# A two-layer decode kernel: output weights of layer 0's last pairs loaded behind the values, the output product one pair behind, the MLP loads recut, no tile context

## The chip, the cores and the metric

The kernel runs on one core of one Trainium2 chip. The metric is the device time of one execution in microseconds (us). Comparisons are between medians of several runs of each kernel; the profile is one execution, recorded by the hardware profiler.

## The reference

Two layers with the same weights, each attention and then an MLP, for one token:

```python
x = A_x                                     # 1 x 1 x 640, bf16
for layer in range(2):
    # attention: 32 heads of 192; of 32768 cached keys the last W = 4096 count
    h = layernorm(x)
    q = (h @ wq) per head                   # wq: 640 x 6144
    p = softmax(q @ k[:, -W:].T * 192**-0.5)
    x = x + concat(p @ v[:, -W:]) @ wo      # wo: 6144 x 640
    # MLP: 1536 wide
    h = layernorm(x)
    x = x + (sigmoid(h @ w_gate) * (h @ w_up)) @ w_down
```

## The kernel before

Work goes by pairs of heads, 16 pairs in each layer. On the host the tensors are laid out so that a pair needs two loads of the same size, 128 rows of 28416 bytes (3552 KB): `a` (from `ua`) holds the pair's query weights and keys, `b` (from `ub`) its values (the first `VE` columns, 3072 KB) and its output weights (the last `WOE` columns, 480 KB). SBUF has seven slots of that size and one region of 3072 KB (`mreg`), which holds MLP weights in the first MLP and the last, and the values of pair 1 in between.

One pair in `step(p, prev)`: `Q` (query projection, L351), `QK` (scores, L366), the softmax (`soft`, `expo`), then for the pair before `PVmm` (values, L420), and `PVout`: a turn of the result (L435), its scaling on DVE (L438, to `oTb`) and the product with the output weights (L445), which adds to `yT`. `ET` (L396 to L405) turns the exponentials of the new pair. In layer 0 the middle of this is a loop of seven turns with two pairs each; in layer 1 the first pairs have an order written out by hand.

Not everything is loaded twice. In layer 0 the loads of pairs 0, 14 and 15 and the keys of pair 1 go to slots that are kept (`KEPT`), and layer 1 begins with these pairs (14, 15, 0, 1), so that its first work needs few new bytes.

All big loads go out on SP's queue, in one fixed order, `seq`. For a layer it is a0, a1, b0, a2, b1, a3, b2 and so on; the last pair's values come in three parts (`b1`, then `b0` twice). Behind layer 0 come the MLP's weights (gate in two parts `wg`, up in two parts `u1`, `u2`, down in two `d1`, `d2`), the values of pair 1 for layer 1 in three parts (`va`, `vb`, `vc`), the keys of layer 1's pair 2 in two parts (`a0`), pair 1's output weights (`wom`) and then layer 1's pairs. While the program is written, `prefetch` puts loads on SP as far as it can: it stops at the first entry of `seq` whose slot is still busy or whose event has not been written yet. Each load waits on SP for the last readers of what it overwrites, and everything behind it on SP waits too.

In layer 0 the keys of pair p go to slot p % 2 and the values to slot 2 + p % 2, apart from the kept pairs 0 and 1 (keys to 4 and 6, values of 0 to slot 5). A key slot comes free at the end of `QK`, a value slot at the end of `PVout`:

```python
            elif not (l == 0 and ("b", p) in KEPT):
                release(sv)
```

`emit` and `emit_pe` write each engine's instructions with their semaphore waits. After the block of all engines come a clearing of semaphores, a barrier and `finish`, which makes the last product as its weights land, writes the output and clears six semaphores on SP. All of it is inside a tile context and a critical section of it.

Of the kernel before, what the change touches and what calls it, by code (L numbers as in the profile page):

```python
# [9 lines left out]
ALU = mybir.AluOpType  # L10
# [34 lines left out]
class _Prog:  # L45

    def __init__(self):
        self.ops = {e: [] for e in ("pe", "dve", "act", "dma", "adma")}
        self.cnt = {e: 0 for e in ("pe", "dve", "act")}
        self.dcnt = {}  # L50
        self.seg = None
# [55 lines left out]
def decode_kernel(ctx: ExitStack, tc: tile.TileContext, cx: bass.AP, ua: bass.AP, ub: bass.AP,  # L107
                  wg_d: bass.AP, wu_d: bass.AP, wd_d: bass.AP, out: bass.AP):
    nc = tc.nc
# [3 lines left out]
    ctx.enter_context(tc.tile_critical(name="decode", no_gpsimd_drain=True))  # L113
# [24 lines left out]
    sh = sb("sh", [P, 6 * DC + 4 + FC], BF16)  # L138
# [3 lines left out]
    oTb = sh[:, 6 * DC:6 * DC + 3]  # L142
    hT = sh[:, 6 * DC + 4:6 * DC + 4 + FC]
# [26 lines left out]
    rm = {n: res("m_" + n) for n in "abc"}  # L170
    MOFF = {"a": (0, 5 * FW), "b": (5 * FW, 12 * FW), "c": (12 * FW, ME)}
# [32 lines left out]
    seq += [("wg", 0), ("wg", 1), ("u1",), ("u2",), ("d1",), ("d2",), ("va",), ("vb",), ("vc",)]  # L204
    tail = stream(1, range(2, 14))
    assert tail[0] == ("a", 1, 2)
    seq += [("a0", 0), ("a0", 1), ("wom",)] + tail[1:]
    seq += [("fg",), ("fu",), ("fd", 0), ("fd", 1), ("fd", 2)]
    seq_pos = [0]
    busy = set()  # L210
# [3 lines left out]
    GH = 5  # L214
# [10 lines left out]
    def try_load(it):  # L225
        k = it[0]
        if k in ("a", "b"):
            s = (A_SLOT if k == "a" else B_SLOT)[it[1]][it[2]]
            if not take(s):
                return False  # L230
            pg.dma(q_dma(slot(s, 0, UNIT), (ua if k == "a" else ub)[it[2]]), f"s{s}", wr=[rslot[s]])
        elif k == "b1":
            s = B_SLOT[it[1]][it[2]]
            if not take(s):
                return False
            n = len(pg.ops["dma"])
            pg.dma(q_dma(slot(s, NB * DH, UNIT - NB * DH), ub[it[2]][:, NB * DH:]), f"s{s}", wr=[rslot[s]])
            ev_done["b1"] = list(pg.ops["dma"][n]["deps"].items())
        elif k == "b0":
            s = B_SLOT[it[1]][it[2]]  # L240
            o = it[3] * NHALF
            pg.dma(q_dma(slot(s, o, NHALF), ub[it[2]][:, o:o + NHALF]), f"bh{it[3]}", wr=[res(f"bh{it[3]}")], extra=ev_done["b1"])
        elif k == "a0":
            if f"a14_{it[1]}" not in ev_done:
                return False
            s = A_SLOT[1][2]
            o0, o1 = ((0, A0CUT), (A0CUT, UNIT))[it[1]]
            pg.dma(q_dma(slot(s, o0, o1 - o0), ua[2][:, o0:o1]), f"a0{it[1]}", wr=[res(f"a0{it[1]}")] + ([rslot[s]] if it[1] else []),
                   extra=[ev_done[f"a14_{it[1]}"]])
        elif k == "wg":  # L250
            f0, f1 = ((0, GH), (GH, FC))[it[1]]
            pg.dma(q_dma(mreg(f0 * FW, (f1 - f0) * FW), wg_d[:, f0 * FW:f1 * FW]), f"wg{it[1]}", wr=[[rm["a"]], [rm["b"]]][it[1]])
        elif k == "u1":
            pg.dma(q_dma(mreg(12 * FW, 7 * FW), wu_d[:, 0:7 * FW]), "u1", wr=[rm["c"]])
        elif k == "u2":
            if "gate0" not in ev_done:
                return False
            pg.dma(q_dma(mreg(0, 5 * FW), wu_d[:, 7 * FW:]), "u2", wr=[rm["a"]])
        elif k == "d1":
            if "gate1" not in ev_done:  # L260
                return False
            pg.dma(q_dma(mreg(5 * FW, 7 * FW), wdp(0, 7)), "d1", wr=[rm["b"]], extra=[ev_done["gate0"]])
        elif k == "d2":
            if "up0" not in ev_done:
                return False
            pg.dma(q_dma(mreg(12 * FW, 5 * FW), wdp(7, 12)), "d2", wr=[rm["c"]])
        elif k in ("va", "vb", "vc"):
            if "down0" not in ev_done:
                return False
            o0, o1 = MOFF[k[1]]  # L270
            pg.dma(q_dma(mreg(o0, o1 - o0), ub[PM][:, o0:o1]), k, wr=[rm[k[1]]])
        elif k == "wom":
            if "QM" not in ev_done:
                return False
            pg.dma(q_dma(slot(A_SLOT[1][PM], 0, WOE), ub[PM][:, VE:UNIT]), "wom", wr=[res("wom")], extra=[ev_done["QM"]])
        elif k == "fg":
            pg.dma(q_dma(mreg(0, 12 * FW), wg_d), "fg", wr=[rm["a"], rm["b"], rm["c"]])
        elif k == "fu":
            if not take(U_SLOT):
                return False  # L280
            pg.dma(q_dma(slot(U_SLOT, 0, 12 * FW), wu_d), f"s{U_SLOT}", wr=[rslot[U_SLOT]])
        else:
            if it[1] == 0 and not take(D_SLOT):
                return False
            c0, c1 = WFIN[it[1]]
            pg.dma(q_dma(slot(D_SLOT, c0 * D, (c1 - c0) * D), wdp(c0, c1)), f"wf{it[1]}", wr=[rslot[D_SLOT]] if it[1] == 0 else [])
        return True
# [50 lines left out]
    def attention(l, xi):  # L338
# [6 lines left out]
        def Q(p, y):  # L345
            sa = A_SLOT[l][p]

            def f(t):
                for i, c0 in enumerate((0, P, 2 * P)):
                    for c in range(DC):  # L350
                        ins = t.matmul(qe[:, i:i + 1], lhsT=slot(sa, c * 2 * DH + c0, P), rhs=xq[:, c:c + 1], start=(c == 0), stop=(c == DC - 1))  # L351
                return ins
            ev = pg.op("pe", f, rd=[res("xq"), rslot[sa]] + ([res("a00")] if l == 1 and p == 2 else []), ex=[rb[3]])
            pg.op("dve", lambda v: v.tensor_tensor(out=qs[:, y], in0=qe[:, 0:3].unsqueeze(2).to_broadcast([P, 3, 32]), in1=mask3, op=ALU.mult),  # L354
                  rd=[res("cst")], wr=[res(f"qs{y}")], ex=[rb[3]])
            return ev
# [51 lines left out]
        def PVmm(p, z):  # L408
# [3 lines left out]
            for h in (1, 0) if half else (0, 1):  # L412
                vt = (mreg(h * NB * DH, NB * DH) if inm else slot(sv, h * NB * DH, NB * DH)).rearrange("p (t d) -> p t d", t=NB)
                for part in (0, 1) if half and h == 0 else (None,):
# [8 lines left out]
                    rV = list(rm.values()) if inm else [rslot[sv]] + ([] if part is None else [res(f"bh{part}")])  # L423
# [4 lines left out]
        def PVout(p, z):  # L428
            inm = l == 1 and p == PM
            sv = None if inm else B_SLOT[l][p]  # L430

            def tm(t):
                for c in range(3):
                    for sg in range(2):
                        ins = t.matmul(oT3[:, c:c + 1], lhsT=o8_sb[:, sg, c:2 * DH:3], rhs=mask2[:, sg:sg + 1], start=(sg == 0), stop=(sg == 1))  # L435
                return ins
            pg.op("pe", tm, rd=[res("o8sb0"), res("o8sb1"), res("cst")], ex=[rb[6]])
            pg.op("dve", lambda v: v.tensor_scalar(out=oTb, in0=oT3[:, 0:3], scalar1=Rn[z], scalar2=None, op0=ALU.mult),  # L438
                  rd=[res(f"Rn{z}0"), res(f"Rn{z}1")], wr=[res("oTb")], ex=[rb[6]])
            wo = slot(A_SLOT[1][PM], 0, WOE) if inm else slot(sv, VE, WOE)  # L440

            def im(t):
                for j in range(DC):
                    for c in range(3):
                        ins = t.matmul(yT[:, j:j + 1], lhsT=wo[:, c * D + j * P:c * D + (j + 1) * P], rhs=oTb[:, c:c + 1],  # L445
# [3 lines left out]
            pg.op("pe", im, rd=[res("oTb")] + ([res("wom"), rslot[sa]] if inm else [rslot[sv]]), ex=[rb[7]])  # L449
            if inm:  # L450
                release(sa)
            elif not (l == 0 and ("b", p) in KEPT):
                release(sv)

# [4 lines left out]
        def step(p, prev):  # L459
# [6 lines left out]
            PVout(prev, prev % 2)  # L466
# [14 lines left out]
        if l == 0:  # L481
# [9 lines left out]
            p = NPAIR - 1  # L491
        else:
            Q(14, 0)
            ln_sq(xi)
            mark("a14_0", QK(14, 0, ks=(0,)))
            mark("a14_1", QK(14, 0, ks=(1, 2)))
            Q(15, 1)
            ln_rstd(K2_ATT, eps_a, srs_c, res("srs"))
            mark("QM", Q(PM, 0))
            QK(15, 1, 1)  # L500
# [3 lines left out]
            Q(0, 1)  # L504
            soft(1)
            expo(1)
            QK(0, 1)
# [6 lines left out]
            QK(PM, 0)  # L514
# [10 lines left out]
            p = 13  # L525
        PVmm(p, p % 2)
        PVout(p, p % 2)
# [10 lines left out]
    def mlp(l, xi):  # L538
# [23 lines left out]
        if last:  # L562
            proj(0, range(FC), g_of, 0, [rm["a"], rm["b"], rm["c"]])
        else:
            mark("gate0", proj(0, range(GH), g_of, 0, [rm["a"]]))
            mark("gate1", proj(0, range(GH, FC), g_of, 0, [rm["b"]]))
# [9 lines left out]
        HS = (0, 7, FC)  # L576
        if last:
            u_of = lambda fb: slot(U_SLOT, fb * FW, FW)
            ru = [[rslot[U_SLOT]]] * 2
        else:  # L580
            u_of = lambda fb: mreg(12 * FW + fb * FW, FW) if fb < 7 else mreg((fb - 7) * FW, FW)
            ru = [[rm["c"]], [rm["a"]]]
        ubank = (1, 6)
        proj(ubank[0], range(0, 7), u_of, 1, ru[0])
        if not last:
            mark("up0")
        proj(ubank[1], range(7, FC), u_of, 1, ru[1], 7)
# [10 lines left out]
        for i in range(2):  # L598
            c0, c1 = HS[i], HS[i + 1]
            wd = mreg((5 if i == 0 else 12) * FW, (c1 - c0) * D)  # L600
# [7 lines left out]
            pg.op("pe", f, rd=[res(f"hT{i}"), rm["b"] if i == 0 else rm["c"]], ex=[rb[7]])  # L608
        mark("down0")
        return residual(xi)  # L610

    def finish():
# [10 lines left out]
        nc.sync.dma_start(out.rearrange("b s (g n) -> (b s g) n", g=NRG), o_row[0:32 * NRG:32]).then_inc(tail_sem["out"], 16)  # L623
        nc.sync.wait_ge(tail_sem["out"], 16)
        for t_ in tail_sem.values():
            nc.sync.sem_clear(t_)
# [90 lines left out]
    with nc.Block() as block:  # L717
# [3 lines left out]

        @block.vector
# [76 lines left out]
```

## Time and profile before

| | before |
|---|---|
| median of 3 runs | 524.4 us (523.97 to 524.91) |
| the profiled execution | 524.21 us |
| its span, first to last instruction | 522.4 us |
| PE matmul busy | 276.6 us (53%) |
| DVE, ACT busy | 97.9 us, 87.9 us |
| SP's load queue | 219.13 MB, 98.5% of 16 engines' time |
| granted TensorE clock, mean | 0.597 |

The span is cut into 40 slices of 13 us for the rows of busy tenths and GB/s. The profile's chain of work that ended last follows each step back to what released it; a DMA stands in it from its issue to its landing, with its time in other loads' wake. The landing of a load is told by 16 marks in the trace, one for each DMA engine; a wait for the load ends with the last of them. L numbers are lines of the kernel of each run.

### The profile page before, as it was taken

The page shows a single profiled execution, that of the slowest core. Times are in us where ns is not written, and L with a number is a line of the kernel's source. Part 1 is how long each engine was busy: PE and PEld are TensorE (multiplying, and loading weights), DVE is VectorE, ACT ScalarE, POOL GpSimd, SP SyncE. Part 2 cuts the span into 40 slices and gives each one's busy share as a digit, 9 for nine tenths or more (in the row PEclk, how much of TensorE's full clock was granted, in tenths as well). Part 3 has the DMA queues.
Part 4 walks back from the last instruction along what each step waited for, and adds up shares of the span by engine and source line. Part 5 has one row for each costly group of instructions (what it writes and reads, how often), then busy time and mean ns, then how long its engine had stood idle before and what let it go on. Part 6 is the DMA issues. An engine that isn't in the chain of part 4 may idle for free.

```text
span 522.4 us, 8445 instructions
## 1 busy us (share of the span) xinstructions
PE 276.6 (53%) x3716; PEld 139.8 (27%) x3716; DVE 97.9 (19%) x372; ACT 87.9 (17%) x171; POOL 0.2 (0%) x4
## 2 busy tenths in 40 slices
PE   0635354544545354545565768677554544545365
PEld 0222122222222122212224434333222222222134
DVE  1212111112011111111111232332211112011111
ACT  0122111210122102210120032222211210122110
POOL 0000000000000000000000000000000000000000
PEclk9967665756665655555555556866666656555555
DMA  8999999999999999999999999999999999999995
GB/s 351 429 434 430 434 428 429 433 429 439 429 425 435 429 435 429 431 435 429 429 415 371 366 440 430 434 423 434 430 429 429 431 433 435 429 429 431 424 426 225
DMA packets 11115, 219.45 MB, mean 420 GB/s; under 512 B 1368, under 2 KB 1368, under 8 KB 2904
## 3 DMA queue, kind: packets, MB, share of 16 engines
q1 hardware_dynamic: 10952, 219.13, 98.5%
q8 instruction: 13, 0.21, 0.2%
q10 hardware_dynamic: 144, 0.06, 0.1%
q14 instruction: 6, 0.05, 0.0%
HBM read 219.18 MB, written 0.00 MB: 420 GB/s over the span
## 4 chain that ended last, share of the span: by engine, by line
DMA 73%; PE 18%; DVE 4%; SPq 1%; issue 1%; ACT 1%; ACTq 0%; DVEq 0%
DMA big<-in_ub_dram 61%; PE o L420 8%; DMA big<-in_wd_dram 7%; DMA big<-in_wu_dram 5%; PE scores L366 3%; PE bank L403 2%; PE bank L445 1%; SPq L182 1%; PE bank L396 1%; ACT e_sb L390 1%; DVE sc L405 1%; PE bank L382 1%; DVE et_sb L400 1%; DVE sc L376 1%; DVE sh L438 1%
## 5 line engine op out<-in xcount | busy, mean ns | idle before, releaser
L420 PE MATMUL o<-big,et_sb 128*2 128x384 bf16 x1024 | 86.3, 511 | 54.8 <-DMA big<-in_ub_dram 54.7
L366 PE MATMUL scores<-big,qs 128*32 128x512 bf16 x744 | 83.8, 620 | 10.3 <-DVE qs L354 9.8
L379 ACT ACTIVATE diag<-cst,sc 128x128 f32<-128x128 bf16 x32 | 12.8, 401 | 263.0 <-DVE sc L376 255.4
L351 PE MATMUL bank<-sh,big 128*128 128x1 bf16 x480 | 17.7, 166 | 71.6 <-DMA big<-in_ua_dram 71.3
L420 PEld LDWEIGHTS o<-big,et_sb 128*2 128x2 bf16 x1024 | 29.2, 113 | 98.6 <-DMA big<-in_ub_dram 63.9
L376 DVE TENSOR_REDUCE sc<-scores 128x1 f32<-128x1024 f32 x31 | 38.0, 1224 | 80.4 <-PE scores L366 80.4
L382 PE MATMUL bank<-diag,sc 128*128 128x128 f32 x64 | 23.3, 462 | 47.9 <-ACT diag L379 47.9
L390 ACT ACTIVATE e_sb<-scores,sc 128x1024 bf16<-128x1024 f32 x31 | 37.3, 1204 | 41.3 <-DVE sc L385 39.4
L425 ACT CAST o_sb<-o 128x384 bf16<-128x384 f32 x64 | 30.4, 477 | 78.0 <-PE o L420 77.9
L366 PEld LDWEIGHTS scores<-big,qs 128*32 128x32 bf16 x744 | 24.2, 134 | 44.4 <-issue 31.4
L351 PEld LDWEIGHTS bank<-sh,big 128*128 128x128 bf16 x480 | 15.7, 105 | 74.6 <-DMA big<-in_ua_dram 73.2
L382 PEld LDWEIGHTS bank<-diag,sc 128*128 128x128 f32 x64 | 14.6, 285 | 73.6 <-ACT diag L379 71.9
L400 DVE CAST et_sb<-bank 128x64 bf16<-128x64 f32 x32 | 7.2, 225 | 127.4 <-PE bank L396 127.4
L354 DVE TENSOR_TENSOR qs<-bank,cst 128x96 bf16<-128x96 f32 x32 | 8.2, 258 | 103.7 <-PE bank L351 103.6
L445 PE MATMUL bank<-sh,big 128*128 128x1 bf16 x480 | 17.4, 165 | 16.4 <-DVE sh L438 16.4
L403 PE MATMUL bank<-sc 128*128 128x2 f32 x64 | 15.5, 312 | 14.5 <-DVE sc L401 14.5
L445 PEld LDWEIGHTS bank<-sh,big 128*128 128x128 bf16 x480 | 14.7, 100 | 19.0 <-DVE sh L438 18.6
L383 DVE TENSOR_REDUCE sc<-bank 128x2 f32<-128x128 f32 x32 | 9.3, 292 | 43.5 <-PE bank L382 43.5
L403 PEld LDWEIGHTS bank<-sc 128*128 128x128 f32 x64 | 12.8, 249 | 17.3 <-DVE sc L401 17.3
L396 PEld LDWEIGHTS bank<-cst,e_sb 128*128 128x128 bf16 x256 | 9.1, 103 | 23.2 <-ACT o_sb L425 16.8
L396 PE MATMUL bank<-cst,e_sb 128*128 128x8 bf16 x256 | 11.9, 170 | 5.6 <-ACT e_sb L390 5.6
L405 DVE RECIPROCAL sc<-bank 64x1 f32<-64x1 f32 x64 | 10.6, 165 | 19.5 <-PE bank L403 18.5
(60 smaller groups left out, 98.5 us busy)
## 6 DMA issues: line engine op xcount, KB each, us to landing
big<-in_ua_dram SPq DMA_DIRECT2D x27, 3552.0 KB, 30.0
big<-in_ub_dram SPq DMA_DIRECT2D x26, 3552.0 KB, 28.5
big<-in_ub_dram SPq DMA_DIRECT2D x2, 2016.0 KB, 16.3
big<-in_ub_dram SPq DMA_DIRECT2D x4, 768.0 KB, 18.5
big<-in_ua_dram SPq DMA_DIRECT2D x1, 2048.0 KB, 12.7
big<-in_wg_dram SPq DMA_DIRECT2D x1, 1920.0 KB, 23.3
big<-in_wu_dram SPq DMA_DIRECT2D x1, 1920.0 KB, 27.4
big<-in_ua_dram SPq DMA_DIRECT2D x1, 1504.0 KB, 8.4
```

Source lines behind the costliest of these rows:

```text
L351: ins = t.matmul(qe[:, i:i + 1], lhsT=slot(sa, c * 2 * DH + c0, P), rhs=xq[:, c:c + 1], start=(c == 0), stop=(c == DC - 1))
L366: ins = t.matmul(sc_x[1 + b][32 * j:32 * j + 32, :], lhsT=qs[:, y, k, :], rhs=slot(sa, WQE + k * W + (4 * b + j) * 512, 512), start=(k == ...
L376: pg.op("dve", lambda v: v.reduce_max(out=mx, in_=sc_x[0][:], axis=AX.X), wr=[res("mx")], ex=sc_x[3:5])
L379: pg.op("act", lambda a: a.mul(out=diag[:], in_=ident, mul=mx), rd=[res("cst"), res("mx")], wr=[res("diag")])
L382: pg.op("pe", lambda t: t.matmul(dmx[:, 0:P], lhsT=ones_f, rhs=diag[:], start=True, stop=True), rd=[res("diag"), res("ones")], ex=[rb[2]])
L390: pg.op("act", lambda a: a.activation(out=e_sb[:], in_=sc_x[0][:], func=ACT.Exp, bias=nbias, scale=srs_c, accum_out=rowsum), rd=[res("nbia ...
L396: ins = t.matmul(qe[:, 0:2 * NB].rearrange("p (r x) -> p r x", r=2)[:, :, 4 * b:4 * b + 4], lhsT=e_sb[:, b * P:(b + 1) * P], rhs=sel, star ...
L403: pg.op("pe", lambda t: t.matmul(dmx[:, P:P + 2], lhsT=ones_f, rhs=rs2, start=True, stop=True), rd=[res("rs2"), res("ones")], ex=[rb[2]])
L405: pg.op("dve", lambda v, h=h: v.reciprocal(out=Rn[z][64 * h:64 * h + 64], in_=dmx[64 * h:64 * h + 64, P + h:P + h + 1]), wr=[res(f"Rn{z}{h ...
L420: ins = t.matmul(o8[h][32 * j:32 * j + 2, 0:2 * DH].rearrange("p (a d) -> p a d", a=2), lhsT=et_sb[:, z, h * NB + 2 * u:h * NB + 2 * u + 2 ...
L425: pg.op("act", lambda a, h=h: a.copy(out=o8_sb[:, :, h * DH:(h + 1) * DH], in_=o8[h][:, 0:2 * DH].rearrange("p (a d) -> p a d", a=2)), wr= ...
L445: ins = t.matmul(yT[:, j:j + 1], lhsT=wo[:, c * D + j * P:c * D + (j + 1) * P], rhs=oTb[:, c:c + 1], start=False, stop=(c == 2), skip_grou ...
```

## The change

What it does:

- `PVout` is split in `PVt` (turn and scaling) and `PVn` (output product and release of the value slot). In layer 0 a step makes `PVt` of the pair before and `PVn` of the pair before that one; in layer 1 both are of the same pair, as now. `oTb` has two buffers.
- The `b` loads of pairs 0, 14 and 15 of layer 0 hold only the values. The output weights of 14 and 15 (`wol`) are loaded behind the last values, ahead of the MLP's. Those of pair 0 (`wo0`) go to slot 2, from where GpSimd copies them to slot 5 for layer 1; slot 2 is marked busy from the start.
- The region of the MLP is tracked in cells of 640 columns (20 of them) in place of three parts. Gate is cut 6 + 6 (was 5 + 7), up 5 + 2 + 5 (was 7 + 5), down 6 + 6 (was 7 + 5), pair 1's values in four parts (were three), each released by its own event.
- In layer 1 the query projection of pair 1 goes to bank 6 and ahead of pair 14's scores; `wom` is loaded ahead of `a0`.
- There is no tile context and no critical section. `finish` clears its semaphores but one before it waits for the output.

```diff
-    ctx.enter_context(tc.tile_critical(name="decode", no_gpsimd_drain=True))
...
-    rm = {n: res("m_" + n) for n in "abc"}
-    MOFF = {"a": (0, 5 * FW), "b": (5 * FW, 12 * FW), "c": (12 * FW, ME)}
+    rc = [res(f"cell{i}") for i in range(-(-ME // FW))]
+    MW = {"wg0": (0, 0, 6), "wg1": (6, 6, 12), "u1": (12, 0, 5), "u2": (17, 5, 7), "u3": (0, 7, 12), "d0": (5, 0, 6), "d1": (11, 6, 12)}
+    MAFTER = {"u3": ("gate0",), "d0": ("gate0", "gate1"), "d1": ("gate1", "up0")}
+    MV = {"v0": (0, 5), "v1": (17, len(rc)), "v2": (5, 11), "v3": (11, 17)}
+    VAFTER = {"v0": "up2", "v1": "up1", "v2": "down0", "v3": "down1"}
...
     seq = stream(0, range(NPAIR))
-    seq += [("wg", 0), ("wg", 1), ("u1",), ("u2",), ("d1",), ("d2",), ("va",), ("vb",), ("vc",)]
+    seq.insert(seq.index(("b", 0, 0)) + 1, ("wo0",))
+    seq += [("wol", 14), ("wol", 15)] + [(k,) for k in (*MW, *MV)]
...
-    seq += [("a0", 0), ("a0", 1), ("wom",)] + tail[1:]
+    seq += [("wom",), ("a0", 0), ("a0", 1)] + tail[1:]
...
-    busy = set()
+    busy = {2}
...
+        elif k == "wo0":
+            s = B_SLOT[0][2]
+            pg.dma(q_dma(slot(s, VE, WOE), ub[0][:, VE:UNIT]), f"s{s}", wr=[rslot[s]])
+        elif k == "wol":
+            s = B_SLOT[0][it[1]]
+            pg.dma(q_dma(slot(s, VE, WOE), ub[it[1]][:, VE:UNIT]), f"wol{it[1]}", wr=[res(f"wol{it[1]}")], extra=ev_done["b1" if it[1] == 15 else "b14"])
...
         def PVout(p, z):
+            PVt(z)
+            PVn(p, z)
+        def PVt(z):
...
+        def PVn(p, z):
+            inm = l == 1 and p == PM
+            sv = None if inm else 2 if l == 0 and p == 0 else B_SLOT[l][p]
...
             elif not (l == 0 and ("b", p) in KEPT):
                 release(sv)
+            if l == 0 and p == 0:
+                pg.op("pool", lambda g: g.tensor_copy(out=slot(5, VE, WOE), in_=slot(2, VE, WOE)), rd=[rslot[2]], wr=[res("wol0")])
+                release(2)
...
             PVmm(prev, prev % 2)
             ET(p % 2)
-            PVout(prev, prev % 2)
+            PVt(prev % 2)
+            n = prev - 1 + l
+            if n >= 0:
+                PVn(n, n % 2)
...
             p = NPAIR - 1
+            PVmm(p, 1)
+            PVt(1)
+            PVn(p - 1, 0)
+            PVn(p, 1)
         else:
             Q(14, 0)
+            mark("QM", Q(PM, 1, 6))
             ln_sq(xi)
...
+        for k in tail_sem:
+            if k != "out":
+                nc.sync.sem_clear(tail_sem[k])
         nc.sync.wait_ge(tail_sem["out"], 16)
-        for t_ in tail_sem.values():
-            nc.sync.sem_clear(t_)
+        nc.sync.sem_clear(tail_sem["out"])
...
-    with _tile.TileContext(nc) as tc:
-        decode_kernel(tc, *args, o)
+    decode_kernel(nc, *args, o)
```

## The prediction

> **What bounds the kernel now.** I read the page first (the 40 slices, the queues, the chain that ended last), then the chain in order of time around one steady pair, SP's issues around the same pair, a table of four-microsecond windows over the first MLP, and the two ends.
>
> ```profile
> DMA  8999999999999999999999999999999999999995
> GB/s 351 429 434 430 434 428 429 433 429 439 429 425 435 429 435 429 431 435 429 429 415 371 366 440 430 434 423 434 430 429 429 431 433 435 429 429 431 424 426 225
> ...
> q1 hardware_dynamic: 10952, 219.13, 98.5%
> ...
> DMA 73%; PE 18%; DVE 4%; SPq 1%; issue 1%; ACT 1%; ACTq 0%; DVEq 0%
> ```
>
> SP's one load queue is busy for 98.5% of the span and the chain is DMA for 73% of it: the time is 219 MB through this queue, plus whatever leaves the queue empty. The bytes stay as they are, so the change can win or lose only where the queue runs dry, and at the two ends. It dips in slices 21 and 22 (371, 366 GB/s). That is the first MLP.
>
> One steady pair of layer 0, from the chain:
>
> ```profile
> 221.77 28.31 DMA big<-in_ub_dram
> 250.09 0.04 issue
> 250.13 2.73 PE o L420 x32
> 252.86 0.32 PE bank L396 x8
> ...
> 253.62 0.60 PE bank L403 x2
> ...
> 254.63 0.24 DVE sh L438
> 254.87 0.05 issue
> 254.92 0.57 PE bank L445 x15
> 255.49 0.02 issue
> 255.51 0.33 SPq L182
> ```
>
> Pair 13's values land at T13 = 221.77 + 28.31 = 250.08. The output product (L445) ends 5.4 later and frees slot 3, and SP issues pair 15's values at 255.51. The chain's same step two pairs earlier starts at 188.05 and takes 28.30, to 216.35; the 33.73 between are 16.87 for a pair and 8.43 for one 3552 KB load: 431 GB/s when the queue is fed.
>
> ```profile
> 228.54 0.33 SPq L182 DMA_DIRECT2D big<-in_ua_dram  x1
> 238.64 18.15 SPq L182 DMA_DIRECT2D big<-in_ub_dram  x4
> 256.83 0.91 SPq L182 DMA_DIRECT2D big<-in_wg_dram  x2
> 257.78 0.43 SPq L182 DMA_DIRECT2D big<-in_wu_dram  x1
> ```
>
> At 255.51 the queue still holds the rest of a15 (issued 228.54) and all of b14 (issued 238.64): 16.87 - 5.43 = 11.4 us of data. That cover is what the change spends.
>
> **The change part by part.**
>
> *Output product a pair behind.* `step` now ends with `PVt(prev)` and `PVn(prev-1)` in layer 0, and `release(sv)` sits in `PVn`. So the slot of b(p) comes free not after its own values are used but after those of p+1: b(p+2) waits for `PVmm(p+1)`, which waits for b(p+1) to land. Queued behind it on SP is a(p+4). The new release is a little quicker: `PVn` needs no `oTb` of this step (L438), so it follows L435 (254.06 to 254.36) directly and ends at about 254.9, 4.85 after the landing instead of 5.43.
> - Steady pairs: when b(p+2) is issued, b(p+1) has landed and only a(p+3) is in the queue, with 8.43 - 4.85 = 3.6 us left. What an issue needs ahead of the end of the queue: the first load of the program, into an empty queue, was issued at 0.96 and landed at 12.42 (Q(0) began at 12.47); 11.46 - 8.43 = 3.0. The first of its 16 landing marks in the trace came at 11.53, 2.1 after the pure transfer. So 3.6 covers it, by 0.6. Price 0 for each of 13 pairs. Bounds: a gain is excluded, since the queue is never faster than fed; one load in the middle (vc, a part of layer 1's kept values) was issued 4.8 ahead of its predecessor's landing and still lost 0.45. I allow up to 0.3 a pair, 0 to +4.
> - The last pair has no a16 behind it. The order is a15, b14, b15. b14 is issued at T13 + 4.85 with a15 ahead of it. a15 lands at T13 + 8.43, b14, now without its 480 KB of output weights, 7.3 later: T14 = T13 + 15.7. b15 needs `PVn(13)`, which stands behind `PVmm(14)` on PE: it is issued at T14 + 4.85, into an empty queue, and wol14, wol15 and all MLP loads stand behind it on SP. So the queue is dry from about 265.8 to 270.6 plus the start of the new load: 4.85 + 3.0 = **+7.85** on the last landing. Bounds for the start: 2.0 (the first landing mark of the refill at 280.2, see below) and 3.8 (its last: 5.7 from issue to landing for 800 KB, of which 1.9 is transfer): +6.85 to +8.65. Nothing hides this: the kernel is bound by the queue before and after.
>
> The Trainium skill, "DMA: Bandwidth & Descriptors", section "Anatomy of one DMA", gives (for GpSimd's path) a fixed cost of about 2.0 us beside bytes/436e3 and calls it nearly constant. By it the gap would be 6.85 and the forecast 1.0 lower. The row of the first load says 3.0 for its last engine, and a consumer waits for all 16.
>
> *MLP loads recut, output weights of pairs 14 and 15 behind the last values.* The windows of before:
>
> ```profile
> 256.00:280.00 24.00, 13.52 (x182) 6.55 (x183) 3.79 (x19) 3.61 (x7) 0.00 (x0) 0.50 0.99 418
> 280.00:284.00 4.00, 2.76 (x80) 2.56 (x77) 0.40 (x2) 0.73 (x3) 0.00 (x0) 0.50 0.82 285
> 284.00:288.00 4.00, 0.88 (x28) 0.74 (x25) 0.45 (x2) 0.00 (x0) 0.00 (x0) 0.50 0.99 392
> 288.00:292.00 4.00, 2.21 (x62) 2.04 (x62) 0.17 (x2) 0.00 (x0) 0.00 (x0) 0.50 0.98 360
> 292.00:296.00 4.00, 3.30 (x41) 1.60 (x41) 0.73 (x6) 0.00 (x0) 0.00 (x0) 0.50 0.97 357
> 296.00:300.00 4.00, 4.00 (x60) 2.17 (x56) 1.78 (x4) 0.87 (x3) 0.00 (x0) 0.50 0.98 367
> ```
>
> Against 431 these five lose (146 + 39 + 71 + 74 + 64) x 4 us = 1.58 MB, 3.7 us. u2 is issued at 280.2, only 2.7 before u1 lands (257.78 + 25.1), and va, vb, vc wait for gate and down products in the same way. After the change each refill has more ahead of it. With X the landing of the last values: wol15 lands at X+2.3, wg0 4.7, wg1 7.0, u1 8.9, u2 9.75. gate0 (30 products, about 0.96 at L558's 60 in 1.96) ends X+5.7, so u3 is issued 4.05 ahead of the end of the queue; d0 (gate1, X+8.0) 3.65, d1 (up0) 4.1, v0 (up2) 3.7, v2 (down0) 4.1, v3 (down1) 4.1, wom 4.2, a00 4.35. All are at or over the 3.0 above. The last output product waits for wol15 and ends 0.4 later after X than now; its cover is that gate0 waits for wg0 anyway.
>
> What of the 3.7 comes back? Three 16 KB instruction packets of queue 8 lie in this stretch (283.1, 294.2, 307.0; 0.9 to 1.0 each), on one of the 16 engines each, and the program must still fetch its code: if the last engine carried all three, only 0.8 is a dry queue. But the first of the 16 landing marks lost as much as the last one between u1 and a3, so most of it is a dry queue. I take **-3.0**, bounds -0.8 and -3.7. The skill's "Runtime: NRT & Kernel Launch", section "Instruction fetch mechanics", has instruction blocks of 16 KiB whose crossing is mostly hidden; by it the whole 3.7 would come back, 0.7 better than I take. No row here separates the two.
>
> Five more small loads: small ones ran at 418 against 431 between 256 and 280, 0.7 us over about nine, 0.08 each: **+0.3** (0.2 to 0.4).
>
> *Pair 0's output weights by way of slot 2.* GpSimd copies them to slot 5 once wo0 lands (about 30); slot 2 is wanted at T1 + 4.85 = 52. ACT copies 128x384 in 0.48 (L425), so 1920 columns are some 2.4 there; even at four times that, 12 us of cover are left. Price 0; if the cover were gone, the copy itself once.
>
> *Layer 1.* The early Q for the kept pair (0.56) moves ahead of QK(14): half a microsecond on a PE that runs beside fed loads (SP's issues there are 8 to 16 ahead). `PVn` there follows its own pair as before. 0.
>
> *No tile context; clears moved.* Start: L113 and L795 stand between 0.67 and the first issue at 0.96; without them **-0.2**. End:
>
> ```profile
> SPq L626 <- DMA out_dram<-o_sb: 1.0, 1, 1.0
> SPq L795 <- PEq L795: 0.5, 2, 0.4
> ```
>
> The output lands at 521.0, the span ends at 522.43. In between are six clears (521.01 to 521.36), L113's and L795's barriers. Five clears move under the 1.0 wait for the output and the barriers go; one clear of 0.04 is left: **-1.4** (-1.2 to -1.6).
>
> Sum: -0.2 + 0.3 + 0 + 7.85 - 3.0 - 1.4 = +3.55. The profiled execution took 524.21 (span 522.43 and 1.8 around it), 0.2 under the median of 524.4: 527.8 on its own base, **528.0** on the median's.
>
> **The rivals.**
> 1. *The gap at b15 does not open, and it is faster.* Were b15 issued while b14 still flows, the rest stands alone: -0.2 + 0.3 - 3.0 - 1.4 = -4.3, 520.1. It decides from a gap of 4.3 us down, that is if b15 is issued earlier than 1.3 after T14. Against it: `PVmm(14)` alone takes 2.73 (L420), and slot 3's last reader, `PVn(13)`, stands behind it. For it: only a misreading of the order of release. 0.09.
> 2. *Every refill in layer 0 costs.* 3.6 us of cover are too few, as vc's 4.8 were, and 13 pairs lose 0.3 each: 528.0 + 3.9 = 532. For it: vc; against it: va, with 3.8 ahead, lost nothing. 0.10.
> 3. *The change does not mend the first MLP*: the stalls go with the instruction packets and stay, only 0.8 comes back: 528.0 + 2.2 = 530.2. 0.11.
>
> **How the numbers follow.** The forecast has 0.70. With all terms at their good ends it gives -0.2 + 0.2 + 6.85 - 3.7 - 1.6 = +1.55, 526.0; I begin the range at 525.5 for the share of rival 1 in which a short gap is left, and end it at 532.0, which takes in rivals 2 and 3. About 1.0 us (0.2%) is what a measurement here can tell from no change. Faster by more: 0.07, the body of rival 1; within: 0.06, its short gap and the forecast's low edge; slower: 0.87.
>
> **What would show it.** SP issues b15 (its first part now 1536 KB) near 270.6 and not 255.5, with DMA share near zero for about five microseconds before 272; b and a issued in pairs, 0.4 apart, 4.8 after each landing of values, 16.87 apart from pair to pair (more means rival 2). From X on the windows should stay near 420 GB/s (if they dip to 360, rival 3). After the output's issue the span should end in 1.7 us instead of 3.1. The forecast is wrong at its root if no hole in the DMA row stands before the last values of layer 0.

## The result, and the profile after

| | before | after |
|---|---|---|
| median | 524.18 us (523.88 to 524.91, 4 runs) | 538.67 us (535.18 to 540.48, 4 runs) |
| ratio to before | | 1.0266, 95% interval 1.0213 to 1.0319 |
| profiled execution, its span | 524.21, 522.4 | 540.48, 539.1 |
| MB moved by SP's queue | 219.13 | 219.13 |

The change is 14.5 us slower. 528.0 was forecast, with a range up to 532.0: the sign and the place were right, the size was not. The profiled execution is the slowest of the four; it is compared below with before's profiled execution.

The rows of 40 slices (13.5 us each) and the chain's share, from the page of after:

```profile
DMA  9999999999999999999949999999999999999996
GB/s 363 418 439 425 408 394 384 423 407 399 426 413 422 415 382 411 430 386 420 409 166 400 412 407 435 431 433 427 429 430 430 433 434 430 426 431 434 425 422 273
...
DMA 69%; PE 22%; DVE 4%; SPq 2%; issue 1%; ACT 1%; ACTq 0%; DVEq 0%
```

Two things are new. One slice has 166 GB/s: the forecast gap. And in slices 5 to 20, from the first refill of layer 0 to the last, the rate is about 410 where it was 430, while the row of DMA shares says 9 throughout. (A refill is a load into a slot that has just come free; in layer 0 here, a values load.) The second is the larger loss, and the share hardly shows it, because a packet counts as busy for as long as it takes, and in layer 0 packets take longer: some 310 are over 1.1 us, against 4 before.

The chain in order of time, from the refill of pair 12 (issued at 229.74) to that of pair 15 (start, duration, what):

```profile
229.74 13.85 DMA big<-in_ub_dram
243.60 0.04 issue
243.64 2.73 PE o L420 x25
...
247.67 0.39 PE bank L450 x15
248.06 0.02 issue
248.08 12.38 DMA big<-in_ub_dram
...
265.16 12.21 DMA big<-in_ub_dram
277.38 0.04 issue
277.42 2.73 PE o L420 x32
...
281.65 0.41 PE bank L450 x15
282.07 0.02 issue
282.08 0.33 SPq L182
```

Every pair now stands in the chain with its own DMA step (before, one step of 28.3 covered two pairs), and the steps differ: 13.85, 12.38. From 229.74 to 248.08 is 18.34 for a pair, where 16.87 was normal. Pair 14's values land at 277.38, and SP issues pair 15's 4.70 later, behind the output product (now L450), into an empty queue. The windows around it (us, busy time and count of each engine, granted clock, DMA share, GB/s):

```profile
272.00:276.00 4.00, 1.89 (x14) 0.67 (x6) 1.52 (x2) 0.40 (x1) 0.00 (x0) 0.50 0.74 313
276.00:280.00 4.00, 2.58 (x32) 0.92 (x32) 0.17 (x2) 1.77 (x3) 0.00 (x0) 0.50 0.01 6
280.00:284.00 4.00, 1.60 (x35) 1.35 (x31) 0.92 (x5) 0.48 (x1) 0.00 (x0) 0.50 0.26 55
284.00:288.00 4.00, 0.00 (x0) 0.00 (x0) 0.00 (x0) 0.00 (x0) 0.00 (x0) 0.50 0.95 392
```

The account, by the last of each load's 16 landing marks:

| | forecast | measured |
|---|---|---|
| start | -0.2 | -0.4 by the landing of a3 (55.25, was 55.66); the first load is issued at 0.74, was 0.96, but lands at 12.35, was 12.42 |
| 13 refills of layer 0 | 0 | +11.4 |
| other loads of layer 0 behind a3 | 0 | +0.6 (the keys loads lose 1.1; before had lost 0.5 at one values load) |
| gap ahead of pair 15's values | +7.85 | +7.15 (277.38 to 288.18, less 3.65 of transfer) |
| five more small loads | +0.3 | about +0.2 (some 0.06 each) |
| first MLP (the last 13376 KB up to the landing of layer 1's a3) | -3.0 | -0.9 (34.72, was 35.62 for the same bytes) |
| end (last landing to end of span) | -1.4 | -1.4 (2.6, was 4.0) |
| sum | +3.55 | +16.65; the spans of the two profiled executions differ by 16.7, their times by 16.27 |

### The profile page after: what moved, and what is told of

The parts are those of the page before. It is cut to its first block, busy times and chain, and to the rows that moved or that the text cites. A ratio compares the mean times of both kernels' runs of the same rounds, so it can differ in the third digit from the quotient of the medians.

```text
span 539.1 us, 8408 instructions
## 1 busy us (share of the span) xinstructions
PE 271.2 (50%) x3716; PEld 137.9 (26%) x3716; DVE 98.0 (18%) x372; ACT 87.7 (16%) x171; POOL 2.0 (0%) x5
## 3 DMA queue, kind: packets, MB, share of 16 engines
q1 hardware_dynamic: 11672, 219.13, 96.9%
## 4 chain that ended last, share of the span: by engine, by line
DMA 69%; PE 22%; DVE 4%; SPq 2%; issue 1%; ACT 1%; ACTq 0%; DVEq 0%
DMA big<-in_ub_dram 59%; PE o L420 12%; DMA big<-in_wd_dram 7%; PE scores L366 3%; DMA big<-in_wu_dram 3%; PE bank L403 2%; PE bank L450 2%; SPq L182 2%; PE bank L396 2%; DVE et_sb L400 1%; ACT e_sb L390 1%; PE bank L382 1%; DVE sc L401 1%; DVE sc L376 1%; PE bank L436 0%
## 5 line engine op out<-in xcount | busy, mean ns | idle before, releaser
L420 PE MATMUL o<-big,et_sb 128*2 128x384 bf16 x1024 | 85.2, 505 | 71.3 <-DMA big<-in_ub_dram 71.3
L420 PEld LDWEIGHTS o<-big,et_sb 128*2 128x2 bf16 x1024 | 29.1, 113 | 113.9 <-DMA big<-in_ub_dram 79.4
L382 PE MATMUL bank<-diag,sc 128*128 128x128 f32 x64 | 21.2, 425 | 47.5 <-ACT diag L379 47.4
L382 PEld LDWEIGHTS bank<-diag,sc 128*128 128x128 f32 x64 | 13.2, 257 | 72.4 <-ACT diag L379 71.8
L403 PE MATMUL bank<-sc 128*128 128x2 f32 x64 | 16.5, 327 | 14.5 <-DVE sc L401 14.5
L450 PE MATMUL bank<-sh,big 128*128 128x1 bf16 x480 | 17.2, 165 | 7.9 <-DVE sh L439 7.6
L450 PEld LDWEIGHTS bank<-sh,big 128*128 128x128 bf16 x480 | 14.9, 101 | 9.2 <-DVE sh L439 8.4
L396 PEld LDWEIGHTS bank<-cst,e_sb 128*128 128x128 bf16 x256 | 9.1, 103 | 23.1 <-ACT o_sb L425 16.8
L396 PE MATMUL bank<-cst,e_sb 128*128 128x8 bf16 x256 | 11.8, 170 | 5.6 <-ACT e_sb L390 5.6
## 6 DMA issues: line engine op xcount, KB each, us to landing
big<-in_ub_dram SPq DMA_DIRECT2D x4, 768.0 KB, 13.5
```

What stands on the lines that cost most here:

```text
L382: pg.op("pe", lambda t: t.matmul(dmx[:, 0:P], lhsT=ones_f, rhs=diag[:], start=True, stop=True), rd=[res("diag"), res("ones")], ex=[rb[2]])
L396: ins = t.matmul(qe[:, 0:2 * NB].rearrange("p (r x) -> p r x", r=2)[:, :, 4 * b:4 * b + 4], lhsT=e_sb[:, b * P:(b + 1) * P], rhs=sel, star ...
L403: pg.op("pe", lambda t: t.matmul(dmx[:, P:P + 2], lhsT=ones_f, rhs=rs2, start=True, stop=True), rd=[res("rs2"), res("ones")], ex=[rb[2]])
L420: ins = t.matmul(o8[h][32 * j:32 * j + 2, 0:2 * DH].rearrange("p (a d) -> p a d", a=2), lhsT=et_sb[:, z, h * NB + 2 * u:h * NB + 2 * u + 2 ...
```

## The experiments

Theory: the late release costs the time, through how much load is left in the queue when the next is issued (its cover). Rivals: the new loads, GpSimd's copy and the smaller cuts cost it; two loads issued together start each other late; a wait at every pair costs by itself. Times of before in the three sessions: 523.95, 524.03, 524.55.

**e1: the release put back, all else of the change kept.** In layer 0 `PVn(prev - 1)` stands at the head of the step, where PE waits for keys anyway.

```diff
         def step(p, prev):
+            if l == 0 and prev >= 1:
+                PVn(prev - 1, (prev - 1) % 2)
             Q(p, 0)
...
             PVt(prev % 2)
-            n = prev - 1 + l
-            if n >= 0:
-                PVn(n, n % 2)
+            if l == 1:
+                PVn(prev, prev % 2)
```

> The changed kernel with one thing undone: in layer 0 the output product of the pair behind stands at the head of the step, ahead of the query projection, and no longer behind the values' product of the next pair. It still runs a pair behind in program order, and the output weights of pairs 14 and 15 still load behind the last values, but a value slot is free about 5.4 us after its own values landed, as in the kernel before. Theory (cover: the loss is the late release, 13 refills with 3.7 us of load left in the queue and one dry gap ahead of pair 15's values): loads of layer 0 land 8.43 us apart again, no gap; 524.2 - 0.2 (start) - 1.4 (end) - 1 to - 3 (first MLP) = 520 to 522. Rival (new loads: GpSimd's copy, the split output weights, the recut and the five further small loads cost the time): stays at 530 or more.

Measured: 521.04 us (520.45 to 521.48), ratio 0.9939 (0.9926 to 0.9953): faster than before, 17.6 under the change. The two rows from its page:

```profile
DMA  8999999999999999999999999999999999999996
GB/s 352 429 437 425 427 437 428 428 437 428 431 435 429 426 437 431 426 437 431 428 411 389 390 439 428 432 428 430 430 431 433 428 431 433 431 429 435 420 428 265
```

No hole, and layer 0 is back at 430. All of the change's loss is in where one group of 15 products stands on PE. GpSimd's copy (1.78 us in after), the late output weights and the small cuts are still here.

**e2: no tile context alone.** The kernel before with the change's lines on the tile context, the critical section and the clears.

> The kernel before with no tile context, no critical section and the clears ahead of the output's wait; nothing else. Theory: the start is 0.2 and the end 1.4 us shorter and both are on the path: 522.6, span 520.8. Rival (what is cut off the end of the span comes back outside it): span 520.8, time 524.2.

Measured: 522.40, ratio 0.9967 (0.9955 to 0.9978), 1.55 under before. The rival falls: nothing that is cut from the span comes back outside it. But the parts are not as forecast. The median span is 1.1 shorter (521.1, was 522.2), not 1.6; the other 0.4 goes outside the span. In the profile the end is 1.4 shorter (2.6 from the last landing, was 4.0), and the start brings nothing that shows: the first load lands at 12.22 to 12.59 in the profiles of the six kernels here without the context, and at 12.29 to 12.70 in those of the seven with it.

**e3: the late release alone.** The kernel before; a value slot's next load waits for one event more.

```diff
+    late, pend = {}, []
+
+    def free_late(ev):
+        while pend:
+            s_ = pend.pop()
+            late[s_] = ev
+            release(s_)
...
-            pg.dma(q_dma(slot(s, 0, UNIT), (ua if k == "a" else ub)[it[2]]), f"s{s}", wr=[rslot[s]])
+            pg.dma(q_dma(slot(s, 0, UNIT), (ua if k == "a" else ub)[it[2]]), f"s{s}", wr=[rslot[s]], extra=[late.pop(s, None)])
...
-            pg.dma(q_dma(slot(s, NB * DH, UNIT - NB * DH), ub[it[2]][:, NB * DH:]), f"s{s}", wr=[rslot[s]])
+            pg.dma(q_dma(slot(s, NB * DH, UNIT - NB * DH), ub[it[2]][:, NB * DH:]), f"s{s}", wr=[rslot[s]], extra=[late.pop(s, None)])
...
-            pg.op("pe", im, rd=[res("oTb")] + ([res("wom"), rslot[sa]] if inm else [rslot[sv]]), ex=[rb[7]])
+            ev_im = pg.op("pe", im, rd=[res("oTb")] + ([res("wom"), rslot[sa]] if inm else [rslot[sv]]), ex=[rb[7]])
+            free_late(ev_im)
...
             elif not (l == 0 and ("b", p) in KEPT):
-                release(sv)
+                if l == 0:
+                    pend.append(sv)
+                else:
+                    release(sv)
```

> The kernel before with one wait more: in layer 0 the load into a value slot waits for the output product of the next pair, too. Loads, slots, cuts, order and context stay as before. Queue cover at each refill is 3.0 us (3.7 in the changed kernel). Theory (cover): the changed kernel's loss in full without any of its other parts: 13 refills at 0.9 to 1.5 and a gap of 5.4 + 2.4 at pair 15: 524.2 + 12 to 19 + 7.8 = 544 to 551. Rival (new loads, copy and recut cost the time; a late release costs only the gap): 532.

Measured: 544.71 (542.38 and 547.03), ratio 1.0394 (1.0351 to 1.0437). The whole loss comes back with none of the other parts.

**e7: late at pair 15 alone** (`if l == 0 and p == 13` in the diff above).

> The kernel before with one wait more at one place: the load of pair 15's values in layer 0 waits for pair 14's output product. Theory: one dry gap of 5.4 + 2.4 us, steady pairs untouched; +7 to +8, of which up to 2 may come back because a dry queue lets the engine that lags catch up: 530 to 532. Rival (the gap is hidden by work that waits anyway in the first MLP): 526 or less.

Measured: 532.44 (531.73 and 533.15), ratio 1.016 (1.014 to 1.0179): +8.5, a little over what was expected. Its load of pair 15 landed 7.7 late, and nothing of it came back. So the gap and the refills are two separate losses, and the gap is the smaller.

**How much cover a refill needs.** e4 and e5 are e3 with another event: the scores of the pair after next (`QK`), and the next pair's values product (`PVmm`).

> The kernel before; in layer 0 the load into a value slot waits for the scores of the pair after next, too, so it is issued with 12.9 us of load left in the queue (20 before, 3.7 in the changed kernel); pair 15's values with 4.4. Theory (cover: an engine that runs dry restarts late; nothing is lost while no engine runs dry): loads of layer 0 land 8.43 us apart, 524 to 525. Rival (a wait at every pair costs by itself, whatever is in the queue): 12 refills at 0.8, 533.

> As the run before, but the added wait is for the next pair's values product: 5.7 us of load left in the queue at each refill of layer 0, and a gap of 2.8 + 2.4 ahead of pair 15's values. Theory (cover): the first of the 16 engines is about 2.4 ahead of the last, so 3.3 is left on it, over the 2.0 to 2.4 of a restart: 0 to 0.3 a refill, 524 + 0 to 4 + 5 = 529 to 533. Rival (the cover needed is over 6): 0.8 each as with 3.0 to 3.7, 524 + 10 + 5 = 539.

Measured: e4 524.30, ratio 1.0009 (0.9997 to 1.0021); e5 529.47, ratio 1.0107 (1.0063 to 1.015). e5's chain:

```profile
202.33 14.05 DMA big<-in_ub_dram
216.38 0.04 issue
216.43 2.73 PE o L427 x32
219.16 0.04 PE bank L403
219.20 14.04 DMA big<-in_ub_dram
```

Here, too, every pair's DMA step is in the chain and SP waits at each, yet a pair takes 16.87 and nothing is lost. That a release is on the chain is not a loss. All of e5's 5.4 us is its gap (10.19 for 4.83 of transfer).

e11 is the change with `PVn(prev - 1)` between `PVmm(prev)` and `ET`; e10 is e3 with the turn of the next pair's result (`tm`) as its event.

> The changed kernel; in layer 0 the output product of the pair behind stands between the values product and the turn of the exponentials, so a value slot is released about 3.4 after the landing instead of 4.8 and each refill has 5.0 us of load left in the queue instead of 3.7. Theory (cover; 5.6 lost nothing, 3.7 lost 0.9 each): refills lose 0 to 0.2 each, the gap at pair 15 is 3.4 + 2.4: 521.0 + 5.8 less a lead of about 1.5 that the dry queue gives back = 525 to 528. If the threshold lies above 5.0: 533 or more.

> The kernel before; in layer 0 the load into a value slot waits for the next pair's turned result (the step ahead of the output product), too: about 4.2 us of load left in the queue at each refill. It places the threshold between 3.7 (0.9 lost each) and 5.6 (none). Gap at pair 15: 4.3 + 2.4. Without loss at the refills: 530 to 531; with 0.8 each: 540.

Measured: e11 527.40, ratio 1.0048 (1.0028 to 1.0068); e10 532.92 (531.96 and 533.88), ratio 1.0156 (1.0119 to 1.0193), between its two cases. e11's chain:

```profile
219.75 13.57 DMA big<-in_ub_dram
233.32 0.04 issue
233.36 2.73 PE o L420 x32
236.09 0.49 PE bank L450 x15
236.58 0.03 PE bank L396 x2
236.61 13.57 DMA big<-in_ub_dram
```

13.57 each time, 16.86 a pair. Against after's chain only the order L420, L450, L396 is new: 1.4 us earlier, and the 11 us at the refills are gone, while a gap (5.2, was 7.15) stays.

e8 lets the queue run wholly dry at twelve pairs: the values load waits for the query projection that uses the keys ahead of it.

> The kernel before; in layer 0 the values loads of pairs 3 to 14 wait for the query projection that uses the keys ahead of them in the queue, so the queue is wholly dry at each. It prices a restart with all 16 engines idle. Theory (all start together and alike, as at pair 15 of the changed kernel: 2.4 from issue to landing over the transfer, marks 0.5 apart): 12 x (0.6 + 2.4) = 36, 560. Rival (a restart takes the 3.7 to 5.5 that the refills show, idle or not): 12 x (0.6 + 4.6) = 62, 586.

Measured: 566.70 (565.94 and 567.47), ratio 1.0817 (1.0754 to 1.0881). The chain:

```profile
215.53 0.33 SPq L182
215.86 0.04 issue
215.90 19.46 DMA big<-in_ua_dram
235.36 0.05 issue
235.41 0.57 PE bank L354 x15
235.99 0.02 issue
236.00 0.33 SPq L182
```

20.47 from issue to issue, 3.6 over a fed pair. All 16 engines start again together: the last mark comes 2.5 to 3.1 after the pure transfer, the 16 of them 0.6 to 1.2 apart.

All of them side by side, from the trace's landing marks and packets of the profiled executions in layer 0. "Left" is the time from the issue to the landing of the load ahead of it, on the last engine and on the first; "loss" is what a values load landed later than its transfer behind that; a normal 28416-byte packet takes 1.054 us, and the long ones are counted among those that start between 50 and 260 us:

| kernel | left, last engine | left, first engine | loss each, mean (range) | packets over 1.1 us, of some 3100 (e8: 2644) |
|---|---|---|---|---|
| before, e1 | 20 | 17 to 18 | 0 (one load of before 0.50) | 4, 3 |
| e4 | 13.1 | 11.0 | 0 | 4 |
| e5 | 5.6 | 3.1 | 0 | 13 |
| e11 | 5.1 | 2.6 to 3.4 | 0 | 46 |
| e10 | 4.1 to 4.4 | 1.7 to 2.9 | 0.16 (0 to 0.75) | 102 |
| after | 3.7 to 4.2 | 0.8 to 1.9 | 0.88 (0 to 1.85) | 310 |
| e3 | 3.0 to 3.3 | -0.1 to 2.1 | 0.78 (0 to 2.28) | 258 |
| e8 | dry by 0.64 | dry | 3.4 (3.1 to 3.7) | 173 |

The edge lies between 4.1 and 5.1 us on the last engine, and it is not sharp: e6, below, lost 0.55 at one refill with 4.60 left and nothing at another with 4.56. The theory stands: the loss goes with the load that is left. What happens on the engines is only in part visible. In the five microseconds behind an issue, at least 14 of the 16 engines have a packet in flight in before, e4 and e5; at after's 13 refills the lowest number is 8 to 14. But a refill's loss does not follow this number (0.97 lost at 14, 0.01 at 10). Summed over layer 0 of after, engines without a packet at the refills account for 65 us of engine time, 4.1 per engine, and packets that take longer than 1.054 for some 120, 7.5 per engine.

**e6: are two loads at once to blame?** In after the keys load follows 0.4 us behind the values load. e6 holds it until the next query projection.

```diff
+            hold = k == "a" and it[1] == 0 and it[2] >= 4
+            if hold and f"Q{it[2] - 1}" not in ev_done:
+                return False
...
-            pg.dma(q_dma(slot(s, 0, n), (ua if k == "a" else ub)[it[2]][:, 0:n]), f"s{s}", wr=[rslot[s]])
+            pg.dma(q_dma(slot(s, 0, n), (ua if k == "a" else ub)[it[2]][:, 0:n]), f"s{s}", wr=[rslot[s]], extra=[ev_done[f"Q{it[2] - 1}"]] if hold else [])
...
+            if l == 0:
+                mark(f"Q{p}", ev)
```

> The changed kernel; in layer 0 the keys load that follows each values load on SP by 0.4 us is held until the next query projection, about 4 us later, so that each values load starts alone. Theory (cover): nothing changes at the values loads, the keys have 7 us of cover: 535 to 540 as the changed kernel. Rival (two loads issued together start each other late): the 11 us at the refills of layer 0 go, 527.

Measured: 536.47 (533.9 and 539.05), ratio 1.024 (1.0029 to 1.0452). Its times overlap after's (535.18 to 540.48), and its refills lose 0.37 each in the one profile, against 0.88. This run alone does not settle it. e5 and e11 issue the two loads 0.37 apart as well, and lose nothing: two loads at once do not cost by themselves. Whether they add to the loss when little load is left stays open.

**e9: what the late output weights bring.** No tile context and the recut, with the output weights loaded with their values and the product on its own pair.

```diff
-    seq.insert(seq.index(("b", 0, 0)) + 1, ("wo0",))
-    seq += [("wol", 14), ("wol", 15)] + [(k,) for k in (*MW, *MV)]
+    seq += [(k,) for k in (*MW, *MV)]
...
-            PVt(prev % 2)
-            n = prev - 1 + l
-            if n >= 0:
-                PVn(n, n % 2)
+            PVout(prev, prev % 2)
```

> The kernel before with no tile context and with the recut of the first MLP (and the order of layer 1 that goes with it); the output weights are loaded with their values as before, and the product follows its own pair. Against the first run (521.04) it lacks only the late output weights, against the second (522.4) it has only the recut. If the recut by itself gives the 1.4 us between those two: 521.0. If it is the 2.3 us of output weights that stand in the queue while the MLP's products release their cells: 522.4.

Measured: 520.88 (520.1 to 521.95), ratio 0.9928 (0.9906 to 0.995). Equal to e1 within the measurement: the late output weights and the product a pair behind bring nothing that shows, the recut brings 1.5 against e2 (2.1 when each is taken against before of its own session). e9 and e1 are both faster than before and after; e9 is the simpler.

## Why the prediction was wrong, point by point

- **The bound and the order of release: right.** The loads' queue bounds the time; the release moved behind the next pair's values, b and a go out 0.4 apart 4.5 to 4.8 after each landing, and pair 15's load finds an empty queue.
- **The steady refills: wrong, and this is the miss.** The step that failed reads "So 3.6 covers it, by 0.6. Price 0 for each of 13 pairs". The 3.6 was right (3.7), the need of 3.0 was not: it came from the program's first load, where all engines start from rest. The 16 engines are 2.4 apart, and I had both marks in hand: of the 3.6 only 1.2 was left on the engine in front. Engines in front run dry while others still stream, and fall back behind the one that had been last: the last mark comes 3.7 to 5.6 after the issue over the pure transfer. At the refill issued at 229.74, a fed engine that had been last would land at 233.46 + 8.43 = 241.89, and seven of the 16 marks came later (the marks do not name their engine). Measured 0.88 each, 11.4 in all, against an upper bound of 4. Why the engines fall so far back is open.
- **Rival 2 had this loss** with a chance of 0.10 and 0.3 a pair. Its evidence, vc, which lost 0.45 with 4.8 ahead of it, was the row that spoke for a price; I set it aside because va, with 3.8, had lost nothing. A loss that scatters from 0 to 1.85 is not refuted by one zero. But vc was a weak row, too: three more refills of before's first MLP, with 4.5 to 4.8 left (the two of down and the first part of a0), lost 0.06 or less, and an instruction packet stands in vc's (294.2). All of them are loads of 1504 KB or less. Before has no 3552 KB load issued behind another with less than 8 left, so its trace had no row that priced these refills.
- **The gap: right, 0.7 too large.** Issue 4.70 after the landing (4.85 forecast), start 2.45 on the last engine (3.0). By the rule of the Trainium skill's "DMA: Bandwidth & Descriptors", section "Anatomy of one DMA", some 2.0 us that hardly vary (given for GpSimd's path; these loads go out on SP), the start would be 2.0; with all engines dry the runs show 2.3 to 3.1, near it. At the refills of after, 3.7 to 5.6, it is neither 2.0 nor constant, and the measurement decides.
- **The first MLP: the term was too large**, -3.0 against -0.9, and -1.8 and -1.9 where no gap stands ahead of it (e1, e9). After's windows there:

```profile
302.00:306.00 4.00, 1.12 (x35) 0.95 (x33) 0.30 (x2) 0.00 (x0) 0.00 (x0) 0.50 1.02 411
306.00:310.00 4.00, 1.24 (x40) 1.16 (x41) 0.15 (x1) 0.00 (x0) 0.00 (x0) 0.50 0.99 404
310.00:314.00 4.00, 3.44 (x70) 2.51 (x71) 1.16 (x9) 0.00 (x0) 0.00 (x0) 0.50 1.05 403
314.00:318.00 4.00, 3.79 (x58) 1.66 (x50) 1.53 (x3) 0.87 (x3) 0.00 (x0) 0.82 1.02 380
```

  The mean of the engines dips by 1.2 us only, as the covers of 4 said. But the last mark slips by 1.3 at u3 and by 1.3 at the second part of a0, where instruction packets of queue 8 stand in the trace at 302.8 and 326.2 (1.07 and 1.04 us). That these delayed the last engine is likely and not shown: the trace does not say on which engine a packet ran. I had this price (0.8 as the lower bound) and took the other end, because the first mark had lost as much as the last. What counts is the last.
- **End: right, -1.4. Start: not shown.** The issue is 0.2 earlier, but the first landing scatters by 0.4 from kernel to kernel (see e2), and its mean moves by only 0.05. That e2 gains 1.55 where 1.6 was forecast is in part luck: 0.4 that no term had falls off outside the span (about 1.4, was 1.8). **GpSimd's copy, the new order of layer 1, the small loads: right** (e1 keeps them all). **Rival 1** (no gap) was wrong, but what it would have been worth, 520.1, is nearly what e1 shows with the gap removed, 521.0.

## What to carry to other kernels

When a change moves the release of a buffer, count the load that is left in the queue at the new issue, on the engine that is in front and not on the one that lands last; below about 5 us on the last engine here (2.6 on the first) refills of 3552 KB began to cost, though the DMA row still said 9. The figure holds for these loads: of ten refills in after's first MLP, of 352 to 2048 KB with 3.8 to 6.5 left, eight lost 0.2 or less. Price a refill by the nearest refill in the trace, of like size and with its scatter, and not by the program's first load; where there is none, leave the price wide. And look for an order of the same work that releases earlier: the same 15 products at the head of the step instead of its end are worth 17.6 us here.

## What had not been expected

- A queue that runs partly dry restarts later, counted from the issue, than one that is wholly dry, though the refill as a whole costs less (0.88 against 3.4). All engines idle: 2.3 to 3.1 us over the transfer on the last engine, marks 0.4 to 1.2 apart (after at pair 15, e7, e8; 2.9 to 3.4 at the program's start). Some engines idle beside others that stream: 3.7 to 5.6 (up to 4.2 of it is the old load on the last engine), with single 28416-byte packets of up to 3.16 us (1.05 is normal) in the first microseconds of the new load; e8, with all engines idle, has them of up to 2.70. Why is open; no run here separates a slow descriptor from a slow read. The Trainium skill's "DMA: Bandwidth & Descriptors", section "Latency and other measured facts", gives an HBM access 0.2 us on average and 2 at high load, which would fit a read that starts among streaming engines; no run here shows it.
- The scatter seems to go into the time: kernels whose refills run partly dry spread over 5 us from run to run (after 535.2 to 540.5, e3 542.4 to 547.0, e6 533.9 to 539.1), e11, with a gap and well-covered refills, over 2.1 in seven runs. With two runs each of e3 and e6, and before itself spreading over 3.4 in 16 runs, this is a hint.
- Lateness on the chain can be free: in e4 and e5 SP waits at every pair and the chain shows it, at no cost to the refills.
